# Seven PSUM banks in turn for a seven-product second layer, and another rule for filling between attention blocks

## The chip, the cores and the metric

The kernel runs on one core of a Trainium2 chip. The metric is the device time of one execution in microseconds (us), lower is better, given as the median of several runs. Engines are named as in the profile: PE (TensorE; PEld is its weight load), ACT (ScalarE), DVE (VectorE), POOL (GpSimd) and SP (SyncE, which here only issues DMAs). SBUF is the on-chip memory, PSUM the accumulator memory of PE with 8 banks of 512 fp32 per partition.

## The reference

Eight batches of eight heads of causal attention (576 tokens, head size 64, 16 extra "beacon" keys that every token sees), then a two-layer network on the 4608 tokens:

```
scores = q @ k_all.T / 8 ; causal mask, beacons free
a = softmax(scores) ; attn = a @ v_all            # (8, 8, 576, 64)
x = attn laid out as (4608 tokens, 512)
h = x @ w_in            # 512 -> 2048
g = max(0.01*h, h)
out = g @ w_out         # 2048 -> 512, fp32
```

All matmuls run in bf16 with fp32 accumulation.

## The kernel before, in words

**Attention.** Work goes by pairs of heads, g = 0 to 31 (four pairs a batch). Pairs 0 to 7 are laid out by hand; from pair 8 on, the scores of all pairs form one long row of columns that is cut into *blocks* of 1536 columns. A block (line 780, matmuls L314) takes 0.77 us on PE; ACT then takes exponentials of it (two on single PSUM banks, L329, then two or three on double banks, L333), and POOL masks the triangles (L289). There are 26 blocks, called S1 to S26 here. Two or three blocks after its scores, a pair's *values* are multiplied (L359) in two halves of 12 and 18 matmuls, each in a PSUM bank of its own that DVE empties with a reciprocal and a multiply (L388, L389) into x_nat. SP then turns x_nat with DMA transposes into xT (x_turn, L417 and L425). Queries and keys come the same way: POOL issues the loads q_nat and k_nat (L171), and SP issues their transposes qT and kT (L179) when they have landed. Every queue is in order: a transpose on SP waits behind an earlier one whose load has not landed.

**Network.** Tokens go in nine chunks of 512. The first layer of a chunk is 16 *up groups* (moe1, L442: four matmuls of 512 columns, then one ACT activation L450 that empties the bank into gT), called U*chunk*.*n*. The second layer of chunk 0 is plain: 16 pieces P0 to P15 (L512). For chunks 1 to 8 it is the seven-product form of a 2 by 2 block product (Strassen and Winograd): with the chunk's g cut into a11, a12, a21, a22 (token half, feature half) and w_out into b11 to b22, the products are 1 = a11·b11, 2 = a12·b21, 3 to 7 with sums of blocks. Sums of w_out are made once (weight_sums); sums of g by DVE for each chunk (token_sums, line 469, issued at L616), a slice of four features at a time while the chunk's up groups run; the last slice has to follow the last up group. u2 = 1 + 6, u3 = u2 + 7, and the outputs are 1 + 2, u3 + 4, u3 + 5 and u2 + 5 + 3. One product for one tile of 128 tokens is a *down group* (moe2, L539: eight matmuls of 256 columns), called D*chunk*.*product* and a or b for the tile; a chunk has 14.

**PSUM.** The pool ps_sc holds two double banks for scores. The other four banks are one pool, ps_one, shared by everything else: the two single score tiles of a block, up groups, values, transposes, and the products. A tile gets the bank of a tile that the program has done with, and PE waits until that tile has been read.

**Order.** The program writes the order of every engine itself (manual_schedule). A list of attention events sorted by a due time (lines 790 to 814) is walked; before each event, fill() emits up and down groups until a target count is reached (lines 820 to 823). The target spreads the groups that can be done before the next chunk becomes ready over the events in between, less KEPT, which are left for later. fill() alternates between one up and one down group where it may do both (`turn`); after a batch is finished (finish, line 678), the next three groups are down groups (`held`). An up group can be emitted once its chunk's pairs are finished, and at most two chunks ahead of the down groups.

Of the kernel before, what the change touches and what calls it, by code (L numbers as in the profile page):

```python
# [8 lines left out]
FP32 = mybir.dt.float32  # L9
# [6 lines left out]
def kernel(  # L16
# [11 lines left out]
    nc = tc.nc  # L28
# [3 lines left out]
    DM = moe_w_in.shape[0]  # L32
# [5 lines left out]
    NF = DF // 128  # L38
    NCH = NTOK // 512
# [42 lines left out]
    opool = ctx.enter_context(tc.tile_pool(name="opool", bufs=2))  # L82
    ps_sc = ctx.enter_context(tc.tile_pool(name="ps_sc", bufs=2, space=bass.MemoryType.PSUM))
    ps_one = ctx.enter_context(tc.tile_pool(name="ps_one", bufs=4, space=bass.MemoryType.PSUM))
# [368 lines left out]
    ADD, SUB = ALU.add, ALU.subtract  # L453

    def weight_sums(part):
        b11, b12 = w_out_sb[:, 0:HF, 0:HD], w_out_sb[:, 0:HF, HD:DM]
        b21, b22 = w_out_sb[:, HF:NF, 0:HD], w_out_sb[:, HF:NF, HD:DM]
        t1, t2, t4 = (w_sum[:, i] for i in range(3))
        tt = nc.vector.tensor_tensor
        if part == 0:  # L460
            tt(out=t1, in0=b12, in1=b11, op=SUB)
            tt(out=t2, in0=b22, in1=t1, op=SUB)
            tt(out=t4, in0=b21, in1=t2, op=SUB)
        else:
            tt(out=b12, in0=b22, in1=b12, op=SUB)
# [17 lines left out]
    def left(i, n, fc, tile):  # L483
        t = slice(tile * 128, (tile + 1) * 128)
        if n == 1:
            return gT[i][:, fc, t]
        if n == 2:
            return gT[i][:, HF + fc, t]
        if n == 7:
            return gT[i][:, fc, HT + tile * 128 : HT + (tile + 1) * 128]  # L490
        if n == 4:
            return gT[i][:, HF + fc, HT + tile * 128 : HT + (tile + 1) * 128]
        return sums[i][{5: 0, 6: 1, 3: 2}[n]][:, fc, t]

    def right(n, fc):
        if n in (5, 6, 4):
            return w_sum[:, (5, 6, 4).index(n), fc]
        fc0, d0 = {1: (0, 0), 2: (HF, 0), 3: (HF, HD), 7: (0, HD)}[n]
        return w_out_sb[:, fc0 + fc, d0 : d0 + HD]

    PRODUCTS = (1, 6, 2, 7, 5, 4, 3)
    banks, parts = {}, {}

    def ND(i):
        return NF if i == 0 else 2 * len(PRODUCTS)

    def moe2_plain(i, t, quarter):
        if quarter == 0:
            banks["a"] = ps_one.tile([128, 512], FP32, name="acc", tag="one")
        acc = banks["a"]  # L510
        for fc in range(quarter * 4, quarter * 4 + 4):
            nc.tensor.matmul(  # L512
                out=acc,
                lhsT=gT[i][:, fc, t * 128 : (t + 1) * 128],
                rhs=w_out_sb[:, fc],
                start=(fc == 0),
                stop=(fc == NF - 1),
            )
        if quarter == 3:
            osb = opool.tile([128, DM], FP32, name="osb", bufs=3)  # L520
            nc.vector.tensor_copy(out=osb, in_=acc)
            nc.sync.dma_start(out=out[i * 512 + t * 128 : i * 512 + (t + 1) * 128], in_=osb)

    def moe2(i, n2):
        if i == 0:
            moe2_plain(i, n2 // 4, n2 % 4)
            if n2 == NF - 1:
                weight_sums(1)
            return
        n, tile = PRODUCTS[n2 // 2], n2 % 2  # L530
        bank = {1: "a", 2: "a", 6: "b", 7: "c", 4: "c", 5: "d", 3: "d"}[n]
        opens = n in (1, 6, 7, 5)
        apart = i == NCH - 1 and bank == "d"
        if opens and (tile == 0 or apart):
            banks[bank, tile] = ps_one.tile([128, 512], FP32, name="acc", tag="one")
        acc = banks[bank, tile if apart else 0]
        lo = 0 if apart else tile * HD
        for fc in range(HF):
            nc.tensor.matmul(  # L539
                out=acc[:, lo : lo + HD],  # L540
                lhsT=left(i, n, fc, tile),
                rhs=right(n, fc),
                start=(opens and lo == 0 and fc == 0),
                stop=(fc == HF - 1),
                skip_group_check=True,
            )
        if apart:
            combine(i, n, acc[:, 0:HD], (tile, tile + 1))
        elif tile == 1:
            combine(i, n, acc, (0, 2))  # L550

    def combine(i, n, acc, tiles):
        lo, hi = tiles[0] * HD, tiles[1] * HD

        def kept(name, bufs=1):
            if lo == 0 or name == "osb":
                parts[name] = opool.tile([128, 512], FP32, name=name, bufs=bufs)
            return parts[name][:, lo:hi]

        def part(name):  # L560
            return parts[name][:, lo:hi]

        tt = nc.vector.tensor_tensor
        if n == 1:
            nc.scalar.copy(out=kept("u2"), in_=acc)
        elif n == 6:
            tt(out=part("u2"), in0=acc, in1=part("u2"), op=ADD)
        elif n == 2:
            c = kept("osb", 3)
            nc.scalar.copy(out=c, in_=acc)  # L570
            store(i, 0, 0, tiles, c)
        elif n == 7:
            tt(out=kept("u3"), in0=acc, in1=part("u2"), op=ADD)  # L573
        elif n == 5:
            c = kept("p5")
            nc.scalar.copy(out=c, in_=acc)
            tt(out=part("u3"), in0=part("u3"), in1=c, op=ADD)
            store(i, 1, 1, tiles, part("u3"))
        elif n == 4:
            c = kept("osb", 3)  # L580
            tt(out=c, in0=acc, in1=part("u2"), op=ADD)
            store(i, 1, 0, tiles, c)
        elif n == 3:
            c = kept("osb", 3)
            tt(out=c, in0=acc, in1=part("u2"), op=ADD)
            store(i, 0, 1, tiles, c)

    def store(i, half, cols, tiles, c):
        t0 = i * 512 + half * HT + tiles[0] * 128
        n = tiles[1] - tiles[0]  # L590
        nc.sync.dma_start(
            out=out[t0 : t0 + n * 128, cols * HD : (cols + 1) * HD].rearrange("(t p) d -> p t d", p=128),
            in_=c.rearrange("p (t d) -> p t d", t=n),
        )

    done1, done2, at2, ready, turn, first_down, held = [0], [0], [0, 0], [0], [0], [0], [0]

    def fill():
        i1, fc = divmod(done1[0], NF)
        i2, n2 = at2  # L600
        can1 = i1 < ready[0] and (i1 < 2 or i2 > i1 - 2)
        can2 = i2 < NCH and i2 < i1 and done1[0] >= first_down[0]
        if held[0] and can2:
            held[0] -= 1
            down()
        elif can1 and (turn[0] == 0 or not can2):
            up()
        elif can2:
            down()
        return can1 or can2  # L610
# [14 lines left out]
    def up():  # L625
        i1, n = divmod(done1[0], NF)
        assert i1 < ready[0]
        fc = n if i1 == 0 else n // 2 + n % 2 * HF
        moe1(i1, fc)
        add_due()  # L630
        done1[0] += 1
        turn[0] = 1
        if i1 and n % (2 * SLICE) == 2 * SLICE - 1:
            due.extend((i1, op) for op in token_sums(i1, n // 2 + 1 - SLICE, n // 2 + 1))

    def down():
        add_due()
        if at2[1] == 2:
            add_all(at2[0])
        moe2(*at2)  # L640
        done2[0] += 1
        at2[1] += 1
        if at2[1] == ND(at2[0]):
            at2[:] = at2[0] + 1, 0
        turn[0] = 0

    def unused(n, cols=128):
        ps = ps_one.tile([128, 512], FP32, name="av", tag="one")
# [16 lines left out]
            )  # L665

    NG = B * NPAIR
    KEPT = 3

    def has(g):  # L670
        return 0 <= g < NG
# [3 lines left out]
    def chunks_with(g):  # L675
        return (g + 1) // NPAIR * S // 512

    def finish(g, eng=0):
        if eng < 2 and g in xs:
            x_transposes(g, (dve, act)[eng])  # L680
        ready[0] = chunks_with(g)
        if g % NPAIR == NPAIR - 1:
            turn[0] = 1
            held[0] = KEPT

    def run(steps):
        for step in steps.split():
# [52 lines left out]
    with order:  # L740
# [43 lines left out]
            for parts in tiles:  # L784
                triangles(parts)

        def has_down():
            return at2[0] < done1[0] // NF

        since = 0  # L790
        events = []
        for g in range(FIRST, NG):
# [24 lines left out]
        for at, _, what, args in events:  # L817
            while w + 2 < len(ends) and at > ends[w + 1]:
                w, d0 = w + 1, done1[0] + done2[0]
            todo = NF * ready[0] + sum(ND(i) for i in range(ready[0])) - KEPT - d0  # L820
            aim = d0 + todo * (at - ends[w]) / (ends[w + 1] - ends[w])
            while done1[0] + done2[0] < aim and fill():
                pass
            if what is block:
                since = done1[0] + done2[0]
            elif what is value and not has_down():
                while done1[0] + done2[0] < since + 4 and fill():
                    pass
            what(*args)
        while at2[0] < NCH:  # L830
# [31 lines left out]
```

## Time and profile before

| what | value |
|---|---|
| time, median of 3 runs | 333.38 us (333.01 to 333.63) |
| the profiled execution | 332.48 us, of which the span 330.8 |
| PE busy | 317.8 us, 96% of the span |
| ACT, POOL, DVE busy | 199.8, 183.2, 132.5 us (60, 55, 40%) |
| granted TensorE clock | 0.999 |
| chain that ended last | PE 76%, DMA 8%, ACT 5%, DVE 4%, POOL 4% |

Busy PE is not PE at its peak: its matmuls overlap, and their ends are modelled. What counts is the distance between the ends of matmuls that follow each other. In a run without waits one of 512 columns comes every 0.22 us and one of 256 every 0.11 us, so that an up group and a down group both take 0.87 us. A *wait* of PE is what is over that.

### The profile page before, as it was taken

What the parts mean: (1) busy time and instruction counts of PE and PEld (TensorE: products, weight loads), DVE (VectorE), ACT (ScalarE), POOL (GpSimd) and SP (SyncE); (2) the same over time, 40 slices, a digit from 0 to 9 for tenths busy, and PEclk for the clock granted to TensorE, in tenths of its full rate; (3) what the DMA queues carried; (4) which work ended last, traced back from release to release, by engine and by line L of the source; (5) the groups of instructions that cost most, each with busy time, mean ns of one, the idle gap of its engine ahead of it and who ended that gap; (6) DMA issues with size and microseconds to landing.
All of it is one profiled execution on the core that took longest, in us unless ns stands there. A gap on an engine that the chain in (4) does not pass through costs nothing.

```text
span 330.8 us, 8482 instructions
## 1 busy us (share of the span) xinstructions
PE 317.8 (96%) x3401; PEld 213.1 (64%) x3429; DVE 132.5 (40%) x280; ACT 199.8 (60%) x336; POOL 183.2 (55%) x354
## 2 busy tenths in 40 slices
PE   8999999999899999999999999998999999999996
PEld 5574555455586557844778888655875695466685
DVE  3572357126443145414621453334442642333343
ACT  4969861678665784578645865587458514644420
POOL 8895968979987884669546976686221000000000
PEclk9999999999999999999999999999999999999999
DMA  8999999999999999999989999999431113000113
GB/s 134 140 204 178 153 209 121 179 181 131 180 111 169 158 157 142 131 164 102 145 122 154 109 146 113 184 120 155 55 100 37 36 21 127 2 0 34 64 43 117
DMA packets 155929, 39.93 MB, mean 121 GB/s; under 512 B 143041, under 2 KB 153153, under 8 KB 155889
## 3 DMA queue, kind: packets, MB, share of 16 engines
q0 software_dynamic: 99824, 18.54, 83.1%
q1 hardware_dynamic: 55792, 20.77, 38.7%
q8 instruction: 27, 0.44, 0.6%
q14 instruction: 14, 0.11, 0.1%
q10 hardware_dynamic: 272, 0.07, 0.1%
HBM read 37.22 MB, written 9.44 MB: 141 GB/s over the span
## 4 chain that ended last, share of the span: by engine, by line
PE 76%; DMA 8%; ACT 5%; DVE 4%; POOL 4%; issue 2%; SPq 0%; ACTq 0%; POOLq 0%
PE acc L442 34%; PE acc L539 25%; PE av L359 7%; PE sc L314 5%; DMA w_out_sb<-in_moe_w_out_dram 4%; PE acc L512 4%; DMA v_aug<-in_v_dram 3%; DVE gsum L616 2%; ACT aT L333 2%; ACT aT L329 2%; ACT gT L450 1%; DVE x_nat L389 1%; POOL gsum L158 1%; DMA xT<-x_nat 1%; POOL v_aug L214 1%
## 5 line engine op out<-in xcount | busy, mean ns | idle before, releaser
L442 PE MATMUL acc<-xT,w_in_sb 128*128 128x512 bf16 (+1 forms) x615 | 134.0, 357 | 1.9 <-DMA xT<-x_nat 0.5
L450 ACT ACTIVATE gT<-acc 128x512 bf16<-128x512 f32 x144 | 83.0, 620 | 56.9 <-PE acc L442 55.4
L442 PEld LDWEIGHTS <-w_in_sb 128*128 128x128 bf16 x640 | 59.6, 98 | 53.6 <-issue 4.3
L289 POOL TENSOR_SCALAR_AFFINE_SELECT aT<-aT 128x256 bf16<-128x256 bf16 (+2 forms) x160 | 59.8, 403 | 60.9 <-ACT aT L329 38.7
L539 PEld LDWEIGHTS <-gT 128*128 128x128 bf16 x512 | 48.9, 98 | 11.2 <-ACT gT L450 2.3
L333 ACT ACTIVATE aT<-sc 128x1024 bf16<-128x1024 f32 (+3 forms) x64 | 51.7, 890 | 0.0
L539 PE MATMUL acc<-w_out_sb,gT 128*128 128x256 bf16 x384 | 47.2, 273 | 1.4 <-ACT gT L450 1.3
L329 ACT ACTIVATE aT<-sc 128x512 bf16<-128x512 f32 (+3 forms) x64 | 28.9, 520 | 25.3 <-PE sc L314 25.3
L359 PEld LDWEIGHTS <-aT 128*128 128x128 bf16 (+1 forms) x960 | 36.6, 98 | 9.3 <-issue 3.0
L539 PEld LDWEIGHTS <-gsum 128*128 128x128 bf16 x384 | 36.1, 98 | 8.8 <-DVE gsum L616 3.3
L359 PE MATMUL av<-v_aug,aT 128*128 128x65 bf16 (+1 forms) x960 | 39.5, 194 | 1.9 <-ACT aT L329 1.6
L214 POOL DMA_DIRECT2D v_aug<-in_v_dram x40 | 34.3, 866 | 4.3 <-DMA w_in_sb<-in_moe_w_in_dram 4.0
L171 POOL DMA_DIRECT2D q_nat<-in_q_dram x48 | 34.9, 734 | 0.7
L171 POOL DMA_DIRECT2D k_nat<-in_k_dram x48 | 34.8, 732 | 0.7 <-DMA w_out_sb<-in_moe_w_out_dram 0.4
L539 PE MATMUL acc<-w_sum,gsum 128*128 128x256 bf16 x256 | 32.9, 273 | 1.8 <-DVE gsum L616 1.7
L616 DVE TENSOR_TENSOR gsum<-gT 128x1024 bf16<-128x1024 bf16 x16 | 11.2, 697 | 53.9 <-ACT gT L450 53.9
L389 DVE TENSOR_TENSOR x_nat<-av,rec 128x384 bf16<-128x384 f32 (+1 forms) x64 | 31.4, 490 | 2.2
L388 DVE RECIPROCAL rec<-av 128x6 f32<-128x6 f32 (+1 forms) x64 | 11.9, 185 | 50.7 <-PE av L359 50.5
L276 ACT ACTIVATE aT<-sc 128x1024 bf16<-128x1024 f32 (+3 forms) x32 | 26.0, 874 | 3.7 <-PE sc L267 1.9
L314 PE MATMUL sc<-qT,kT 64*128 64x80 bf16 (+22 forms) x384 | 22.4, 250 | 1.2 <-PE acc L442 0.5
L314 PEld LDWEIGHTS <-kT 64*128 64x128 bf16 x384 | 13.3, 94 | 11.9 <-issue 8.9
L573 DVE TENSOR_TENSOR u<-acc,u 128x512 f32<-128x512 f32 x8 | 5.5, 691 | 27.2 <-PE acc L539 27.2
(63 smaller groups left out, 221.5 us busy)
## 6 DMA issues: line engine op xcount, KB each, us to landing
out_dram<-osb SPq DMA_DIRECT2D x27, 256.0 KB, 2.8
q_nat<-in_q_dram POOLq DMA_DIRECT2D x48, 72.0 KB, 4.8
k_nat<-in_k_dram POOLq DMA_DIRECT2D x48, 72.0 KB, 5.2
v_aug<-in_v_dram POOLq DMA_DIRECT2D x24, 128.0 KB, 6.4
w_in_sb<-in_moe_w_in_dram POOLq DMA_DIRECT2D x2, 1024.0 KB, 12.3
w_out_sb<-in_moe_w_out_dram POOLq DMA_DIRECT2D x2, 1024.0 KB, 11.6
out_dram<-u SPq DMA_DIRECT2D x7, 256.0 KB, 2.3
gsum<-in_q_dram POOLq DMA_DIRECT2D x8, 144.0 KB, 6.4
```

What stands on the lines that cost most here:

```text
L171: nc.gpsimd.dma_start(out=t[:, :, par], in_=(q, k)[which][b, 2 * hp + par].rearrange("(t p) d -> p t d", p=NR),)
L214: nc.gpsimd.dma_start(out=dst[lo : ROWS[c], c, :, 0:D], in_=v[b, :, OFF[c] : OFF[c] + n].rearrange("h p d -> p h d"),)
L276: nc.scalar.activation(out=aT[:, :, c0 : c0 + w], in_=sc[:, :, 0:w], func=AF.Exp, scale=0.125)
L289: nc.gpsimd.affine_select(out=view, in_=view, compare_op=ALU.is_ge, fill=0.0, base=128 - n if lo == 0 else 0, channel_multiplier=-1, patte ...
L314: nc.tensor.matmul(out=(sc[par] if apart else sc[:, par])[:, at : at + b - a], lhsT=kT[ps_, c * 128 : (c + 1) * 128], rhs=qT[ps_, q0 : q0 ...
L329: nc.scalar.activation(out=probs[g][:, par, lo:hi], in_=sc[par][:, at : at + hi - lo], func=AF.Exp, scale=0.125)
L333: nc.scalar.activation(out=probs[g][:, :, lo:hi], in_=sc[:, :, at : at + hi - lo], func=AF.Exp, scale=0.125)
L359: nc.tensor.matmul(out=avv[:, n, 0 : D + 1], lhsT=aT[0 : ROWS[c], par, a0 : a0 + 128], rhs=va[0 : ROWS[c], c, 2 * hp + par, :], start=(c = ...
L389: nc.vector.tensor_tensor(out=x_nat[:, t0:t1].rearrange("p t e d -> p (t e) d"), in0=avv[:, :, 0:D], in1=rec[:, n0:n1, None].to_broadcast( ...
L442: nc.tensor.matmul(out=acc[:, lo:hi], lhsT=w_in_cols(fc, j), rhs=xT[:, j, x0 : x0 + hi - lo], start=(j == 0), stop=(j == NJ - 1), skip_gro ...
L450: nc.scalar.activation(out=gT[i][:, fc, :], in_=acc, func=AF.Prelu, alpha=0.01)
L539: nc.tensor.matmul(out=acc[:, lo : lo + HD], lhsT=left(i, n, fc, tile), rhs=right(n, fc), start=(opens and lo == 0 and fc == 0), stop=(fc ...
```

## The change

Each product now opens a PSUM bank for its two tiles and is emptied at its end. Before, product 2 was added in PSUM onto product 1, 4 onto 7 and 3 onto 5, so that a bank stayed open over six groups. The adds that PSUM made are now made by DVE, in part after a copy by ACT (the lines of `combine` that go are in the print above). The order of products becomes 1, 4, 6, 2, 7, 5, 3: the first four groups need no sums of g, and the sums must be complete before the fifth group instead of the third. Results are gathered in single buffers p1, p4, p5, u2, u3 (before, osb had three).

The filling rule changes. There is no `turn`: up groups go first wherever they are allowed, except that two down groups (BEHIND) are taken after each block of scores and after a finished batch. The last two down groups of a chunk (LAST) are held back until the next chunk's up groups are all done. Before every half of values, at least three groups must stand since the last block (before: four, and only where no down group was to be had). KEPT goes from 3 to 8.

```diff
-    PRODUCTS = (1, 6, 2, 7, 5, 4, 3)
+    PRODUCTS = (1, 4, 6, 2, 7, 5, 3)
...
-            osb = opool.tile([128, DM], FP32, name="osb", bufs=3)
+            osb = opool.tile([128, DM], FP32, name=("p1", "p4", "p5", "u3")[t], bufs=1)
...
-        bank = {1: "a", 2: "a", 6: "b", 7: "c", 4: "c", 5: "d", 3: "d"}[n]
-        opens = n in (1, 6, 7, 5)
-        apart = i == NCH - 1 and bank == "d"
-        if opens and (tile == 0 or apart):
-            banks[bank, tile] = ps_one.tile([128, 512], FP32, name="acc", tag="one")
-        acc = banks[bank, tile if apart else 0]
+        apart = i == NCH - 1 and n2 >= 10
+        if tile == 0 or apart:
+            banks["p"] = ps_one.tile([128, 512], FP32, name="acc", tag="one")
+        acc = banks["p"]
...
+        if n in (1, 4, 5):
+            nc.scalar.copy(out=part(f"p{n}", True), in_=acc)
+        if n == 6:
+            add(part("u2", True), acc, part("p1"))
         elif n == 2:
+            add(part("p1"), acc, part("p1"))
+            store(i, 0, 0, tiles, part("p1"))
         elif n == 7:
+            add(part("u3", True), acc, part("u2"))
+            add(part("p4"), part("u3"), part("p4"))
+            store(i, 1, 0, tiles, part("p4"))
         elif n == 5:
+            add(part("u3"), part("u3"), part("p5"))
             store(i, 1, 1, tiles, part("u3"))
+            add(part("p5"), part("u2"), part("p5"))
         elif n == 3:
+            add(part("p5"), acc, part("p5"))
+            store(i, 0, 1, tiles, part("p5"))
...
+    LAST, BEHIND = 2, 2
+
     def fill():
         i1, fc = divmod(done1[0], NF)
         i2, n2 = at2
         can1 = i1 < ready[0] and (i1 < 2 or i2 > i1 - 2)
         can2 = i2 < NCH and i2 < i1 and done1[0] >= first_down[0]
-        if held[0] and can2:
-            held[0] -= 1
+        kept = can1 and i1 == i2 + 1 and ND(i2) - n2 <= LAST
+        if first[0] and can2 and not kept:
+            first[0] -= 1
             down()
-        elif can1 and (turn[0] == 0 or not can2):
+        elif can1:
             up()
         elif can2:
             down()
...
-        if at2[1] == 2:
+        if at2[1] == 4:
             add_all(at2[0])
...
-    KEPT = 3
+    KEPT = 8
...
         if g % NPAIR == NPAIR - 1:
-            turn[0] = 1
-            held[0] = KEPT
+            first[0] = BEHIND
...
             if what is block:
                 since = done1[0] + done2[0]
-            elif what is value and not has_down():
-                while done1[0] + done2[0] < since + 4 and fill():
+                first[0] = BEHIND
+            elif what is value:
+                while done1[0] + done2[0] < since + 3 and fill():
                     pass
```

## The prediction

> **What bounds the kernel.** I read the page first, then the waits of PE, then timelines round the longest waits. PE is the bound, and its clock never falls:
>
> ```profile
> PE 317.8 (96%) x3401; PEld 213.1 (64%) x3429; DVE 132.5 (40%) x280; ACT 199.8 (60%) x336; POOL 183.2 (55%) x354
> ...
> POOL 8895968979987884669546976686221000000000
> PEclk9999999999999999999999999999999999999999
> ```
>
> The change leaves PE's matmuls as they are, in number and shape; only waits can come or go. But the POOL row counts too: it is 8 to 9 tenths busy until about 105 us (slice 13), so the early attention hangs on POOL's loads as well. PE's waits:
>
> ```profile
> PE acc L539 <- DVE gsum L616: 1.7, 5, 0.6
> PE av L359 <- ACT aT L329: 1.6, 3, 0.8
> PE acc L539 <- ACT gT L450: 1.3, 2, 0.7
> ...
> PE acc L442 <- DMA xT<-x_nat: 0.5, 1, 0.5
> PE sc L314 <- DMA kT<-k_nat: 0.4, 1, 0.4
> ```
>
> These are short because a modelled matmul end hides part of each wait. From end to end, less 0.11 us for 256 columns and 0.22 for 512, the waits after 106 us are: product 6 on sums at 126.5, 160.6, 196.7, 231.3, 264.5 and 317.4 (0.73, 0.35, 0.45, 0.73, 0.35, 0.14, together 2.75); values straight behind a block, on a bank that the exponentials have not left, at 162.2 and 170.3 (0.70 + 0.97 = 1.67); product 1 on the last activation at 124.4 and 228.6 (0.31 + 0.85 = 1.16); scores on keys at 121.1 (0.52). **Sum 6.1 us.** This line shows one:
>
> ```profile
> 171.08 0.53 PE L359 MATMUL av<-v_aug,aT 128*128 128x65 bf16 x12 [0.80 <-ACT aT L329]
> ```
>
> **What the change removes.** In its emitted order product 6 stands behind four down groups of its chunk (3.5 us; four sums of 0.69 are 2.8), products 1 of chunks 2 to 8 stand behind at least two other groups, and every value half behind three. So all but the 0.52 go by construction. The 0.52 came from SP's backlog after 100 us; in the new order pair 17's keys have some 5 us of slack, so I count it too. Lower bound 5.2 (some sums still late), I take 6.1.
>
> **What it adds on DVE and ACT.** Seventeen more adds, from seven instead of five a chunk (three more in the last, which is split). A row for SBUF inputs alone (L577) is 0.69 us, the same as from PSUM: 11.5 us on a DVE that is 40% busy. ACT's copies stay three a chunk. Behind an add stand value evictions and sums; the bank that waits is next wanted two or more groups (1.7 us) later, so I take 0; uncovered, at 0.2 us for each, 3 us. The last instruction is the same half-width add, so the tail does not move. After the last value 10 groups instead of 11 stand before U7.0, and two adds (1.4) precede its reciprocal; the last transposes landed at 272.9 for a use at 275.8, so 0.6 us of slack stays: 0.
>
> **New waits behind scores.** After a block ACT is away for 3.5 us:
>
> ```profile
> 113.20 1.08 ACT L329 ACTIVATE aT<-sc 128x512 bf16<-128x512 f32 x2
> 114.15 1.96 ACT L333 ACTIVATE aT<-sc 128x1024 bf16<-128x1024 f32 x2
> 115.96 2.11 ACT L450 ACTIVATE gT<-acc 128x512 bf16<-128x512 f32 x4
> ```
>
> The block began at 112.60, exponentials end at 116.1, and the first bank filled after it is read by 116.6, 4.1 us after the block's start with the hand-over. With four groups between, values come at 4.2: no wait. With three, the fourth bank user stands at 0.77 + 3 × 0.87 + 0.36 (first value half) = 3.7 and waits 0.4 if its bank was that first one. Following the banks through the new program, that is so behind S9, S10, S18, S20 and S23, and 0.25 behind S14. **Sum 2.3 us**; below 0 nothing speaks for, above, twice as much if ACT's copies push further: 1.2 to 4.6.
>
> **The early attention.** Here I expect the loss. KEPT 8 takes five groups out of the first window, and the two reserved groups move more. Emitted round the first up group of chunk 2:
>
> ```
> before  S7 5a 5b v 4a 4b v 3a 3b S8 U2.0
> after   S7 6a 6b 2a v 2b v 7a U2.0 S8
> ```
>
> So when U2.0 starts, five down groups and S8 that were behind PE are still ahead: 5 × 0.87 + 0.77 = 5.1 us. Would it start 5.1 us earlier? It needs the transposes of pair 11:
>
> ```profile
> 96.48 1.22 SPq L179 DMA_TRANSPOSE qT<-q_nat  x1
> 99.25 1.20 SPq L179 DMA_TRANSPOSE kT<-k_nat  x1
> 100.54 1.83 SPq L417 DMA_TRANSPOSE xT<-x_nat  x1
> 102.42 1.22 SPq L425 DMA_TRANSPOSE xT<-x_nat  x1
> ```
> ```profile
> 106.19 2.10 PE L442 MATMUL acc<-xT,w_in_sb 128*128 128x512 bf16 x8 [0.53 <-DMA xT<-x_nat]
> ```
>
> Pair 11's x_nat was ready at 95, but SP stood at the keys of pair 15, loaded late:
>
> ```profile
> 86.78 2.66 POOL L289 TENSOR_SCALAR_AFFINE_SELECT aT<-aT 128x256 bf16<-128x256 bf16 x5
> 89.39 1.47 POOL L171 DMA_DIRECT2D q_nat<-in_q_dram  x2
> 90.84 0.73 POOL L214 DMA_DIRECT2D v_aug<-in_v_dram  x1
> 91.56 0.22 POOL L229 COPY kT<-bkT 128x16 bf16<-128x16 bf16 x1
> 91.69 1.45 POOL L171 DMA_DIRECT2D k_nat<-in_k_dram  x2
> ```
>
> They landed at 98.6 and 99.2, the transposes of x at 106.15, and U2.0's fourth matmul started at 106.19. The new program has the same loads and masks in the same order on POOL and the same order of keys and x on SP. From S4's masks (78.5) to the keys' load POOL waited for ACT only 0.44 + 0.25 us, so an earlier PE can pull this load by 0.7. Against it, the store of P12 to P15 (256 KB, 2.8 us in its row) moves from 78.9 to just ahead of pair 15's transposes on SP: I give it 0.5. Before that, S1 is pinned by its keys (landed 59.94, start 60.03), S2 and S3 have the same groups ahead, S4 and S6 two and one fewer, S7 waits for pair 14's keys (96.1). From there five groups, two values (0.9) and three matmuls bring PE to 102.6. I take 105.9 for the landing, a wait of 3.3 us. **Loss: 5.1 − (106.15 − 105.9) = 4.9 us.** Bounds: no wait (102.6) loses 1.6; a landing at 107.5 loses 6.5.
>
> [...] The trace's clock row is flat, and its longest wait of PE is under 1 us. [...]
>
> **Sum.** 4.9 + 2.3 − 6.1 = +1.1 us. Against the profiled execution, 332.48 us (span 330.8 and 1.7 round it), that is 333.6; the median, 333.38, lies 0.9 above the profiled one, so on its scale the forecast is **334.5 us**.
>
> **Rivals.** 0.2% is 0.67 us, about what a measurement of this kernel can tell from no change.
>
> *Pinned (forecast).* Spread of the landing ±1 us and of the new waits ±1: −0.7 to +3, the middle at 334.5. Chance 0.5.
>
> *Loads come along (faster).* If the transposes of pair 11 land by 102.6, since the DMA queues are emptier when stores are spread, the loss is 1.6 and the sum 1.6 + 2.3 − 6.1 = −2.2: 331.2 us; with the new waits at 1.2, 330.1. It decides below a landing at 104.8, where the sum is 0. For it: unloaded transposes land 2.3 us after issue (256.3 to 258.6), these took 3.7 to 5. Against it: POOL has no idle time to give. Chance 0.27.
>
> *Waits move into ACT (slower).* If every block behind which only three groups stand costs 0.8 instead of 0.4, and the landing is 107.5, the sum is 6.5 + 4.6 − 6.1 = +5: 338.4 us. For it: ACT is 60% busy and its order is fixed. Against it: the second bank user finds its bank free. Chance 0.15.
>
> *The banks do nothing.* The waits named on sums stay because DVE, with its added work, is late just there, so that only 2.8 of 6.1 (values and product 1) go: +4.4, 337.8 us. Against it: DVE is idle 60%. Chance 0.08.
>
> **Numbers.** The forecast's part of 0.5 splits about 0.03 faster, 0.14 same, 0.33 slower; the faster rival 0.22, 0.05, 0; the others are slower. So faster 0.25, same 0.19, slower 0.56. The range leaves out a tenth at each end: 331.0 to 337.8.
>
> **What would show it.** In the new profile: a wait of 2 to 4 us before L442 on xT near 103 to 106, and scores on keys at 94 to 96; no waits of products on sums or on L450; value waits of 0.4 us behind six blocks. If U2.0 starts near 102 without a wait, the pin was wrong, and the kernel is faster. If new waits on ACT add up to over 4 us, that term was too small.

## The result, and the profile after

The changed kernel takes **335.06 us** (median of 12 runs, 332.87 to 338.36), the kernel before on the same chip 332.94 (12 runs, 332.00 to 334.27). The ratio is 1.0059, with an interval of 1.0037 to 1.0081: slower by some 2 us. (Ratios here leave disturbed executions out; medians do not.) The profiled execution took 335.01 us, its span is 333.3 against 330.8: 2.5 us more.

The first page of after, the rows that answer to those of before:

```profile
PE 321.3 (96%) x3429; PEld 214.4 (64%) x3429; DVE 143.6 (43%) x297; ACT 201.6 (60%) x336; POOL 185.6 (56%) x354
...
PEclk9999999799998999999999999999999999999999
```

PE's instructions are the same 3429, but two digits of the clock row are below 9 (a 7 and an 8): there TensorE's clock was granted only in part. Before had none. The list of PE's waits:

```profile
PE acc L442 <- DMA xT<-x_nat: 1.9, 1, 1.9
PE sc L314 <- DMA kT<-k_nat: 1.6, 1, 1.6
PE av L359 <- ACT gT L450: 1.3, 3, 0.6
...
PE acc L442 <- ACT gT L450: 0.4, 2, 0.2
```

No line speaks of products (L537 is now their matmul) that wait on sums or on an activation, and none of values that wait on exponentials (L329): those waits are gone. In their place stand one long wait of the first layer on xT, and one of scores on keys (S1's, at 61 us). PE round the first:

```profile
103.11 0.81 PE L442 MATMUL acc<-xT,w_in_sb 128*128 128x512 bf16 x3
105.78 0.38 PE L442 MATMUL acc<-xT,w_in_sb 128*128 128x512 bf16 x1 [1.85 <-DMA xT<-x_nat]
106.08 1.24 PE L314 MATMUL sc<-qT,kT 64*128 64x272 bf16 x16
107.25 1.89 PE L537 MATMUL acc<-w_out_sb,gT 128*128 128x256 bf16 x8
```

The group at 103.11 is U2.0. Three of its matmuls run, the fourth stands until 105.78. S8 follows, and then the two down groups D1.7b and D1.5a, which take 1.8 and 1.2 us here, not 0.87 each. SP in the same stretch:

```profile
98.60 1.20 SPq L179 DMA_TRANSPOSE kT<-k_nat  x1
99.89 1.22 SPq L417 DMA_TRANSPOSE xT<-x_nat  x1
101.16 1.22 SPq L425 DMA_TRANSPOSE xT<-x_nat  x1
```

The keys of pair 15 hold up the two transposes of pair 11's x behind them, as before: U2.0 goes on at 105.78, and went on at 106.19 before. The order of PE has moved, the transposes have not. Two stretches of after, cut where the clock changes (columns: stretch, its length, busy us of PE, PEld, DVE, ACT and POOL with the number of instructions, the granted clock, then the DMA share and GB/s):

```profile
58.57:61.99 3.42, 1.35 (x15) 0.42 (x12) 1.20 (x3) 0.89 (x2) 3.42 (x5) 1.00 2.00 165
61.99:65.40 3.41, 3.41 (x12) 1.16 (x9) 0.00 (x0) 2.63 (x4) 3.41 (x7) 0.50 1.79 199
65.40:68.81 3.41, 3.41 (x29) 1.61 (x28) 0.00 (x0) 2.07 (x6) 2.53 (x5) 1.00 1.87 181
...
102.95:106.36 3.41, 1.56 (x15) 0.69 (x15) 0.17 (x1) 0.17 (x1) 1.85 (x4) 1.00 1.56 122
106.36:109.77 3.41, 3.41 (x28) 2.27 (x23) 0.59 (x1) 3.30 (x6) 1.64 (x5) 0.50 1.32 194
109.77:113.18 3.41, 3.41 (x30) 1.94 (x28) 1.55 (x4) 1.20 (x2) 3.41 (x6) 1.00 0.67 85
```

PE is busy 1.35 us of the stretch from 58.57 (the rest is a wait of S1 for its keys and one of U1.0 just ahead) and 1.56 us of that from 102.95 (the wait of U2.0). After each comes one stretch of 3.41 us at half clock (0.50), in which PE loses 1.7 us (an estimate, half of 3.41; what the distances of matmul ends exceed 0.22 and 0.11 by adds up to 1.76 and 1.56 in the two). By their mean clock, nine of the twelve executions had one such stretch (0.994 or 0.995) and two had two of them, the profiled one (0.990) among these.

### The profile page after: what moved, and what is told of

Its sections match the earlier page's. It is cut to its first block, busy times and chain, and to the rows that moved or that the text cites. A ratio compares the mean times of both kernels' runs of the same rounds, so it can differ in the third digit from the quotient of the medians.

```text
span 333.3 us, 8536 instructions
## 1 busy us (share of the span) xinstructions
PE 321.3 (96%) x3429; PEld 214.4 (64%) x3429; DVE 143.6 (43%) x297; ACT 201.6 (60%) x336; POOL 185.6 (56%) x354
## 4 chain that ended last, share of the span: by engine, by line
PE 73%; DMA 11%; ACT 6%; POOL 5%; DVE 2%; issue 1%; SPq 1%; DVEq 0%; ACTq 0%; POOLq 0%
PE acc L442 29%; PE acc L537 27%; PE av L359 7%; PE sc L314 6%; DMA k_nat<-in_k_dram 4%; ACT aT L333 4%; DMA v_aug<-in_v_dram 3%; PE acc L512 3%; DMA out_dram<-p 2%; DMA kT<-k_nat 2%; DMA xT<-x_nat 1%; ACT aT L329 1%; POOL gsum L158 1%; POOL v_aug L214 1%; ACT gT L450 1%
## 5 line engine op out<-in xcount | busy, mean ns | idle before, releaser
L450 ACT ACTIVATE gT<-acc 128x512 bf16<-128x512 f32 x144 | 84.8, 609 | 67.1 <-PE acc L442 66.0
L442 PEld LDWEIGHTS <-w_in_sb 128*128 128x128 bf16 x640 | 59.8, 98 | 54.9 <-issue 3.6
L289 POOL TENSOR_SCALAR_AFFINE_SELECT aT<-aT 128x256 bf16<-128x256 bf16 (+2 forms) x160 | 61.7, 413 | 57.5 <-ACT aT L329 35.3
L537 PEld LDWEIGHTS <-gT 128*128 128x128 bf16 x512 | 49.2, 98 | 7.9 <-issue 0.8
L537 PE MATMUL acc<-w_out_sb,gT 128*128 128x256 bf16 x384 | 47.6, 276 | 0.0
L537 PEld LDWEIGHTS <-gsum 128*128 128x128 bf16 x384 | 36.8, 98 | 6.3 <-issue 1.3
L329 ACT ACTIVATE aT<-sc 128x512 bf16<-128x512 f32 (+3 forms) x64 | 28.9, 520 | 14.2 <-PE sc L314 14.2
L562 ACT COPY p<-acc 128x512 f32<-128x512 f32 (+1 forms) x25 | 14.6, 582 | 35.3 <-PE acc L537 33.2
L537 PE MATMUL acc<-w_sum,gsum 128*128 128x256 bf16 x256 | 32.0, 275 | 0.0
```

The lines of the kernel that those rows point to most:

```text
L289: nc.gpsimd.affine_select(out=view, in_=view, compare_op=ALU.is_ge, fill=0.0, base=128 - n if lo == 0 else 0, channel_multiplier=-1, patte ...
L329: nc.scalar.activation(out=probs[g][:, par, lo:hi], in_=sc[par][:, at : at + hi - lo], func=AF.Exp, scale=0.125)
L442: nc.tensor.matmul(out=acc[:, lo:hi], lhsT=w_in_cols(fc, j), rhs=xT[:, j, x0 : x0 + hi - lo], start=(j == 0), stop=(j == NJ - 1), skip_gro ...
L450: nc.scalar.activation(out=gT[i][:, fc, :], in_=acc, func=AF.Prelu, alpha=0.01)
L537: nc.tensor.matmul(out=acc[:, lo : lo + HD], lhsT=left(i, n, fc, tile), rhs=right(n, fc), start=(lo == 0 and fc == 0), stop=(fc == HF - 1) ...
```

## The experiments

Twelve kernels ran on three chips (e1 to e4, e5 to e10, e11 to e14), each time beside the kernel before, whose medians there were 334.06, 333.59 and 332.90 us. So ratios to before are compared across chips, and medians on one.

| run | edit | median us | ratio to before (interval) |
|---|---|---|---|
| e1 | after, KEPT 3 | 336.09 | 1.0052 (1.0013 to 1.0091) |
| e2 | after, pair 11's x first on SP | 332.06 | 0.9919 (0.9881 to 0.9956) |
| e3 | after, unused matmuls in U2.0's wait | 332.97 | 0.9970 (0.9930 to 1.0009) |
| e4 | before, KEPT 8, and `held` with it | 333.92 | 0.9999 (0.9965 to 1.0033) |
| e5 | new products, old filling rule | 329.56 | 0.9851 (0.9786 to 0.9916) |
| e7 | before, pair 11's x first on SP | 332.39 | 0.9975 (0.9943 to 1.0007) |
| e9 | e2, four groups ahead of values | 332.49 | 0.9951 (0.9914 to 0.9989) |
| e10 | e9, KEPT 5 | 329.79 | 0.9862 (0.9807 to 0.9916) |
| e11 | old products, new filling rule | 347.41 | 1.0458 (1.0415 to 1.0500) |
| e12 | e5, pair 11's x first on SP | 327.18 | 0.9851 (0.9814 to 0.9888) |
| e13 | e5, later features last | 327.47 | 0.9857 (0.9818 to 0.9896) |
| e14 | e12 and e13 together | 325.92 | 0.9801 (0.9765 to 0.9838) |

My theory after the result: the order puts U2.0 ahead of its transposes because of KEPT 8, and pays a wait and a half clock for it. Rivals: another part of the rule puts it there; the products' added work costs.

**e1 and e4: KEPT.** In before a finished batch sets `held[0] = KEPT`, so e4 raises two things, the reserve and the number of down groups behind a batch; e1 changes the reserve alone.

```diff
-    KEPT = 8      # e1: after with 3; e4: before with 8
+    KEPT = 3
```

> The changed kernel with KEPT = 3 instead of 8, nothing else. In the emitted order U2.0 then stands behind three more down groups (2.6 us of work). Pinned theory (the loss is that PE reaches the first up group of chunk 2 before the transposes of pair 11 have landed): the wait on xT at U2.0 falls from 1.9 us to under 0.5, the half-clock stretch behind it goes, and the time falls by 2.5 to 4 us against the changed kernel, to about 331.5, below the kernel before. Rival (the loss comes from the added adds and the waits of values behind scores): those stay, so the time stays within 0.7 us of the changed kernel's 335.

> The kernel before with KEPT = 8 instead of 3, nothing else: old products, old rule. All of chunk 1's down groups and S8 still stand ahead of U2.0, but S8 has five groups (4.4 us) less ahead of it, and pair 15's keys land when they did (104). Pinned theory: the scores wait on keys by 3 to 4 us in all at S7 and S8 (and the clock may halve once, 1.7), so the time grows by 3 to 5 us over the kernel before. Rival (KEPT does no harm by itself; the products or the rule do): within 0.7 us of the kernel before.

Both missed, from both sides. e1 is not faster than before, and the wait has grown:

```profile
101.05 0.81 PE L442 MATMUL acc<-xT,w_in_sb 128*128 128x512 bf16 x3
104.54 1.01 PE L442 MATMUL acc<-xT,w_in_sb 128*128 128x512 bf16 x2 [2.69 <-DMA xT<-x_nat]
```

The 2.69 us before the fourth matmul are U2.0's wait again. With KEPT 3, three more down groups stand ahead of U2.0 and two are still to come (five in after), but U2.0 still stands ahead of S8. PE came to it at 101.05 all the same, earlier than in after, and x landed only at 104.5.

The time hides what KEPT does, and the waits show it. Take the work that PE still has to do at 112 us, each matmul at its distance in a run without waits. Against before, after has lost 6.6 us by then and e1 2.7. Of these 3.9 us, 2.6 are the three groups, and 1.2 come from a landing at 104.5, not 105.7. But e1 gets less back: waits over 0.25 us behind 106 us, from end to end, add up to 3.2 us in it, to 1.9 in after and to 5.9 in before. (e1's profiled execution took 333.35 us, 2.7 less than its median; what the others lost is not shown.)

In e4 U2.0 stands behind all of chunk 1's down groups and S8 and has no wait for xT, and the time is that of before. But its longest waits are others:

```profile
PE sc L314 <- DMA kT<-k_nat: 2.8, 2, 1.9
PE acc L539 <- DVE gsum L616: 1.7, 1, 1.7
```

From 55 to 106 us its waits add up to 5.5 us against 3.4 in before, behind 106 us to 1.8 against 5.9. (1.4 of the early difference is S1's wait for its keys. S1 starts at 59.5 to 61.5 us in these profiles, and at 61.4 and 59.8 in e5 and e12, which are alike up to there; so that part need not be KEPT's.) So in these two profiles a larger reserve goes with more lost early and less late, and the two about cancel.

Where U2.0 stands can be followed in the program; these orders were not run. Before with KEPT 8 and `held` at 3 has U2.0 right behind S8 with five down groups of chunk 1 to come, as many as after. Without `turn`, the order of before round U2.0 stays as it is. With two down groups behind a finished batch, not three, U2.0 stands ahead of S8 in before too; with three, not two, it stands behind S8 in after. So my theory holds in part: KEPT 8 sets how much work is left behind U2.0, BEHIND = 2 puts S8 there too, and the wait for x is there with KEPT 3 as well.

**e2 and e7: the place of the transposes.** The transposes of pair 11's x go on SP ahead of queries and keys of pair 15, in after and in before:

```diff
-                events.append((g - 1.75, 0, run, ("T%d" % g,)))
+                events.append((g - (1.55 if g == 15 else 1.75), 0, run, ("T%d" % g,)))
```

> The changed kernel with one thing moved: on SP the transposes of pair 15's queries and keys are issued behind, not ahead of, the transposes of pair 11's x. Work, groups and KEPT are as in the changed kernel. Pinned theory: x of pair 11 is ready at about 96 and lands by 101, so the wait at U2.0 (1.9 us) and the half clock behind it (1.7 us) go; pair 15's keys come at most 1 us later; time falls by 2 to 3.5 us. Rival: SP's order is not what holds U2.0 (the queues are just full), the wait stays, time the same within 0.7 us.

> The kernel before, with one edit: the transposes of x for pair 11 are issued on SP ahead of those of queries and keys of pair 15, as in the run e2. A control: if the edit is good only because the changed order asks for that x early, then before gains no more than its wait at the first up group of chunk 2, 0 to 0.7 us. If it gains 2 us or more, the edit is a plain improvement that says nothing about the change.

SP in e2, and PE behind it:

```profile
95.60 1.20 SPq L417 DMA_TRANSPOSE xT<-x_nat  x1
96.85 1.22 SPq L425 DMA_TRANSPOSE xT<-x_nat  x1
98.24 1.21 SPq L179 DMA_TRANSPOSE qT<-q_nat  x1
99.55 1.21 SPq L179 DMA_TRANSPOSE kT<-k_nat  x1
```

```profile
102.43 1.03 PE L442 MATMUL acc<-xT,w_in_sb 128*128 128x512 bf16 x4
...
104.91 0.45 PE L314 MATMUL sc<-qT,kT 64*128 64x128 bf16 x6 [0.96 <-DMA kT<-k_nat]
```

The x transposes are issued 4.3 us earlier than in after, U2.0 runs its four matmuls at 102.43 without a stop, and the clock stays at 1.0 in this profile (two of the other eleven executions show 0.995). S8 now waits 1.1 us for the keys that were pushed back. By the ratios e2 lies 1.4% below after (4.7 us, 3.2 to 6.1 by the two intervals), more than I expected, and below before; the profiled spans differ by 3.2, and the work left at 112 us by 3.1. In before the same edit is worth 0.25%, an interval that still holds zero: the x is wanted early only by the changed order.

**e3: the clock.** Work that nobody needs fills the wait:

```diff
+        if (i1, n) == (2, 0):
+            unused(8, 512)
```

> The changed kernel with eight unused matmuls of 512 columns (1.75 us at full clock) ahead of U2.0, where PE waited 1.9 us. They compute nothing that is used. Clock theory (a good part of the loss is the 3.4 us at half clock that follow the wait, worth 1.7 us): the clock stays at 1.0 behind U2.0 and time falls by 1.2 to 1.7 us against the changed kernel. Rival (the clock record does not matter, only the wait does): the matmuls fill a wait that is there anyway and the time stays, or grows by up to 0.3 us.

```profile
102.65 1.89 PE L646 MATMUL av<-blank 128*128 128x512 bf16 x8
104.38 1.11 PE L442 MATMUL acc<-xT,w_in_sb 128*128 128x512 bf16 x4
```

The eight matmuls stand where the wait stood. The ratio falls from 1.0059 to 0.9970, 3 us by its middle (1.5 to 4.5 by the two intervals). The half clock is gone from the profile, and all 12 executions show a mean clock of 0.998 or more, while 11 of after's 12 show 0.995 or less. The profiled spans differ by 2.3 us: 1.7 is one stretch at half clock, and 0.7 is the last of x, which landed at 105.07 here and at 105.73 in after, though the edit does not touch it. What more there is in the 3 us, if it is real, this run does not show.

**e5 and e11: the two halves of the change.** e5 has the products of after and `fill`, `up`, KEPT and the target of before; e11 the reverse.

```diff
     # e5, against before (with combine and PRODUCTS of after)
-        if at2[1] == 2:
+        if at2[1] == 4:
             add_all(at2[0])
```

> The changed products, banks and sums (product order 1, 4, 6, 2, 7, 5, 3), under the filling rule of before (alternating, held groups, 3 in reserve). Theory A, the loss of the change comes from the filling rule, which puts the first up group of chunk 2 ahead of its transposes, and not from the products: here that up group stands behind all down groups of chunk 1 and behind S8 again, so it waits under 0.7 us and the clock does not fall; the five waits of products on sums (2.75 us) go; value halves straight behind a block and product 1 on the last activation may stay (up to 2.8 us). 330 to 332 us, 2 to 3 us below before on the same chip. Theory B, the added adds on DVE and the copies on ACT have a price that my sum put at 0: new waits on DVE or ACT of 2 to 3 us, and the time is that of before or above.

> The other half of the change: the products, banks and sums of before (five adds a chunk, banks open over six groups), under the filling rule of after. Theory A, the rule is what costs, and costs it without the new products too: the first up group of chunk 2 waits for its transposes for 2 us or more, the clock is granted at half for 3.4 us at least once, and the time is that of after or above it, 334.5 to 338 us on this chip, 5 us or more over the run e5. Theory B, the loss comes only of the two halves together (banks that open more often under up groups that go first): at or below before, no half clock.

PE in the first page of e5:

```profile
PE 317.9 (97%) x3429; PEld 212.9 (65%) x3429; DVE 142.7 (44%) x297; ACT 199.8 (61%) x336; POOL 184.6 (56%) x354
```

Its waits of PE, the lines on products and on x (total, times, longest):

```profile
PE acc L537 <- ACT gT L450: 2.0, 3, 0.7
...
PE acc L442 <- DMA xT<-x_nat: 0.7, 1, 0.7
```

The four longest of PE's waits in e11:

```profile
PE acc L442 <- DMA xT<-x_nat: 3.3, 1, 3.3
PE acc L442 <- ACT gT L450: 3.2, 9, 0.7
PE av L359 <- ACT gT L450: 2.9, 6, 0.6
PE sc L314 <- ACT gT L450: 2.9, 7, 0.5
```

In e5 all waits on sums (2.75 us) are gone, and those of values straight behind a block too, which I had left open; U2.0 waits 0.82 us from end to end, a little more than I had, and product 1 on the last activation three times (0.81, 0.85, 0.85). The seventeen added adds appear in no wait. That is theory A of its expectation, and the gain is larger than I put it: 1.5%, or 4.9 us (0.8 to 2.1% by its interval); 3.4 in the spans. e11 is dearer than I expected by some 10 us. By the work left, it has lost 8 us to before at 112 us, and 16 at the end. Its nine, six and seven waits on L450 (9.0 us together) I read as waits for a bank: in its emitted order the bank that product 5 of chunk 1 opens (D1.5a, ahead of U2.0) is closed by D1.3b, behind U2.15, so that sixteen up groups have a bank less, and an up group or a score tile comes to one that ACT has not emptied. Its U2.0 waits 3.7 us and is followed by two half-clock stretches. So the two halves do not add: the rule costs 4.6% with the old products and about 2% with the new ones; the products gain 1.5% under the old rule, and 3.8% under the new. The whole change is a good half and a bad one.

**e9 and e10: can the new rule be mended?**

```diff
-                while done1[0] + done2[0] < since + 3 and fill():
+                while done1[0] + done2[0] < since + (3 if done2[0] > downs else 4) and fill():
```

> The run e2 with one more edit: ahead of a half of values stand four groups since the last block, not three, unless one of the groups since was a down group. If the waits of values behind blocks with up groups alone (0.77 and 0.69 us at S4 and S5, some 0.3 each at three later blocks) are the price of the minimum of three, they go and the time falls 0.5 to 1.5 us below e2. If the wait only moves to the next reader of a bank that ACT has not left, the time is that of e2.

> The run e9 with 5 groups in reserve, not 8. The first up group of chunk 2 then stands some three groups later, and S7 and S8 have more groups ahead of them. If the two waits of scores on keys (1.25 and 1.12 us in e2) come from PE being early there, 1 to 2 us less than e9; if PE is only as early again by the groups that are taken from later windows, no change from e9, or up to 1 us more for waits after 106 us.

e9's waits of values behind S4 and S5 are gone, but an up group there now waits 0.77 us for L450, and S4 and S6 wait 1.07 us (for keys) and 1.14 (for DVE): nothing gained over e2, the second outcome. e10 lies 2.7 us below e9 on the same chip, but I can't say why: the waits between 55 and 130 us add up to 6.7 us in e9 and 6.3 in e10 (S7's on keys, 1.27, goes, and S8's grows to 1.20), and the profiled spans differ by 1.1. Three of e9's executions show a mean clock under 0.997, none of e10's. What KEPT costs once the wait for x is gone stays open.

**e12, e13, e14: what is left in e5.** e12 is e2's edit on e5; e13 makes feature 7, which product 1 needs, before the last block rather than behind it; e14 has both.

```diff
-        fc = n if i1 == 0 else n // 2 + n % 2 * HF
+        fc = n if i1 == 0 else {13: 7, 14: 14}.get(n, n // 2 + n % 2 * HF)
```

> The run e5 with the transposes of x for pair 11 ahead of those of queries and keys of pair 15 on SP, as in e2. In e5 the first up group of chunk 2 still waits 0.82 us for them; in the run e7 this wait went and 0.34 us on the next block's keys came in its place. So 0.3 to 0.8 us below e5, and no more: the 2 to 3 us that the edit gave after cannot come again, as this order does not ask for the x early.

> The run e5 with another order of the last four up groups of a chunk: features 6, 7, 14, 15 instead of 6, 14, 7, 15. In e5 the eighth matmul of product 1 needs feature 7, whose up group stands behind a block, so that its activation waits for the exponentials: 0.81, 0.85 and 0.85 us at chunks 1, 2 and 5. With feature 7 ahead of the block these three waits go: 2 to 2.5 us below e5, 327 to 328 us. If ACT is the limit there and not the place of feature 7, the wait moves to product 4 (which needs features 14 and 15) two groups later, and the gain is under 1 us.

> The edits of e12 and e13 on e5 together. If both waits are on the path that sets the end, the gains add: 2.5 to 3.3 us below e5, about 326 to 327 us, below every version so far.

The profiles do what was expected: no wait for xT in e12 (0.41 on keys instead), none of products on L450 in e13. The ratios of e12 and e13 equal that of e5 (0.985), whose own interval is 1.3% wide and from another chip; so the gain of each alone stays open; the 2 to 2.5 us expected of e13 do not show in it. On one chip the median of e14 lies 1.3 us below e12 and 1.6 below e13, where the six runs of one kernel spread by 2 to 3 us. **e14, 325.92 us, is the fastest of all**, 2.0% below before (1.6 to 2.4). The first row of its page:

```profile
PE 316.4 (98%) x3429; PEld 212.5 (66%) x3429; DVE 142.7 (44%) x297; ACT 199.3 (62%) x336; POOL 184.1 (57%) x354
```

The list of its waits begins with one ahead of the first matmuls, on a blank tile:

```profile
PE av L643 <- DVE blank L735: 1.1, 1, 1.1
PE sc L314 <- DVE x_nat L389: 0.5, 1, 0.5
```

PE is busy 98% of the span, and no wait of a group, a product or a block is over 0.7 us from end to end.

## Why the prediction was right, and where it was not

The forecast (334.5, slower) was right in sign and near in size. In part that is luck: it saw 1.1 us between the two kernels, the medians show 2.1, and before came out 0.4 lower in twelve runs than in the three that the forecast started from. Its steps:

- *Removed waits, 6.1 us: right.* After 106 us none of them is left. But I gave them to the change as a whole. e5 and e11 show that either half alone removes the waits on sums, and that the products alone also remove those of values; the new rule was needed only for product 1. In e4, with neither, a reserve and `held` of 8 leave no wait on sums over 0.25 us behind 106.
- *DVE and ACT, 0: right.* e5 has the same adds and no wait on them. In after two short ones appear (0.31 behind a copy, 0.27 behind an eviction).
- *New waits, 2.3 us: nearly right in size (1.9), wrong in place.* Six waits after 106 us: 0.31 at 119.5, 0.36 at 127.6, 0.27 at 184.7, 0.29 at 190.6, 0.33 at 197.9 and 0.36 at 228.9. Only two are of values; the others are up groups. Behind S4 and S5 values wait 0.77 and 0.69, which the later pin hides.
- *What would show it.* The wait on xT is where the text looked for it (103.9 to 105.9), and no product waits on sums. The waits of scores on keys at 94 to 96 did not come in after; in e2 one did (1.25 us at 95.6).
- *Early loss, 4.9 us: right in mechanism and size.* U2.0 is pinned by pair 11's transposes; the step "what moves" (5.1 us) held, and the landing came 0.4 earlier (106.19 to 105.78; I had 0.25). That is 4.7. The wait was 2.0 and not 3.3, since PE came there at 103.9, not 102.6 (the terms given, from S7 on, come to 102.8): the longer wait at S1 and the half clock behind it had already taken time inside the pin. The step "KEPT 8 takes five groups out of the first window" holds in the program's order, and with three of them fewer behind U2.0 (e1) less is lost early. What the text did not see is that KEPT 3 brings more waits later, so that e1 is no faster for it.
- *The clock, left out of the sum: the term that was missed.* Before's clock row is flat, and behind its first matmuls no wait there is over 0.97 us, so it could not show what a longer wait costs; the wait of 3.3 us stands in the sum as a wait alone. A wait of 2.0 us was enough: after it the clock stood at 0.50 for 3.41 us. The half clock before 65 us lies inside the pin, the one after 106.36 does not: 1.7 us.

With it the sum is 4.7 + 1.9 + 1.7 − 6.1 = 2.2 us, against 2.5 between the profiled spans and 2.1 between the medians; without, I had 1.1. The work left agrees: after has lost 6.6 us by 112 us, where the sum says 4.7 + 1.7, and gets 4.2 back behind it, as 6.1 − 1.9. The faster rival needed a landing below 104.8; in after the x landed at 105.7 because SP's order is fixed, and e2, which moves that order and lands x at 101.7, is what the rival would have looked like (332.06 beside 334.06).

## What to carry to other kernels

When a change reorders the bound engine, ask for each group that moves ahead whether its inputs move too: the transposes that stood behind another load's on SP's queue did not (U2.0 went on at 105.78, and at 106.19 before), and one edit on that queue was worth some 3 to 5 us here. Take a change of several parts apart before judging it: here new products gained 1.5% and a new filling rule took 2% back, and neither number could be had from the whole. Ask of a reserve what it costs early and what it saves late: e1 and e4 moved both, and the time hid it. And see over how many other groups a product holds its PSUM bank: under the same rule the long holds of e11 came with 9.0 us of waits on L450, which after has 1.7 of.

## What the runs showed of the hardware

I had not expected a clock that falls after so short a wait (2.0 us at U2.0). In the traces of before and after the clock changes only at whole multiples of 3.413 us from the first entry of its record: in after 17, 18, 30, 31 and 97 of them, in before 95. That first entry stands 3.96 us behind the start of the span in after and 5.64 in before, so these windows do not lie at the same place in the two. What seems to count is how much PE waits inside one of them; that is my reading of the few that follow. By the distances of matmul ends, four windows in mid-run were followed by half clock at full speed before. They had 2.39 and 2.12 us of waits (after), 2.47 (e1) and 2.44 (e11). One with 2.08, in e4, was not, and in before and after no other window at full clock has over 1.42 while PE has matmuls to come. The windows in which PE's last matmul ends agree: 2.30 us were left in before's, and half clock followed at once (329.91 us); 1.68 were left in after's, and it followed one window later (335.05). By PE's busy column the emptiest of the four is e1's; below it stands e4's, which kept the clock:

```profile
100.91:104.33 3.42, 0.95 (x13) 0.43 (x10) 1.90 (x4) 0.36 (x1) 2.53 (x5) 1.00 1.22 160
```

```profile
58.52:61.93 3.41, 1.49 (x11) 0.58 (x11) 1.82 (x3) 0.00 (x0) 3.41 (x5) 1.00 1.91 167
```

e4's window holds S1's wait of 2.08 us and cost no clock. By PE's busy column the edge is not sharp: 1.49 us here kept the full clock, 1.56 in after lost it. Windows that were 28 to 46% busy (0.95 of 3.41 us in e1, 1.56 in after) were followed by half clock. The length of a wait alone did not decide it. In e3 waits of 0.60 us (U1.0) and 2.04 us (S1), more than the 0.60 and 1.79 that half clock followed in after, fell into two windows, with 1.60 and 1.36 us of waits, and the mean clock of that execution, 0.998, leaves no room for a stretch of 3.41 us at half. This may be part of the spread between executions; that was not tried.
